# First weights in four loads instead of two, and two fewer late tiles stored in halves, in a 2:4-sparse matmul

## The chip, the cores and the metric

The kernel runs on one core of one Trainium2 chip. The metric is the device time of one execution in microseconds. A core has five engines that run side by side, each with its own list of instructions: TensorE (PE; its weight loads are listed as PEld), VectorE (DVE), ScalarE (ACT), GpSimd (POOL) and SyncE (SP). SyncE and ScalarE also issue DMAs here, each through a queue of its own; the moving of bytes is done by 16 DMA engines that both queues share.

## The reference

Of every four consecutive rows of the weights, in every column, the two of largest magnitude are kept and the other two become zero; then the product with x is formed, and a bias is added.

```python
B, S, D = 16, 512, 1024            # x: B,S,D  w: D,D  b: D, all bf16
wg = w.reshape(D // 4, 4, D)
mag = jnp.abs(wg)
order = jnp.argsort(mag, 1)
thr = jnp.take_along_axis(mag, order[:, 2:3, :], 1)   # second largest of four
wp = (wg * (mag >= thr)).reshape(D, D)
return jnp.einsum("bsd,df->bsf", x, wp) + b
```

## The kernel before

There are 8192 tokens, in 64 tiles of 128 tokens. Each tile needs 16 matmuls of 128x512 (8 blocks of the 1024 inputs, 2 halves of the 1024 outputs), and one tile's result is a row block of 128x1024.

The weights are held as `w_sb[P, G, 4, Dout]`: the partition is the index of a group of four rows, `G` is 2 (inputs 0 to 511 and 512 to 1023), and the axis of length 4 has the four rows of a group, called rows 0 to 3 below. So the four rows that compete lie side by side in a partition, and VectorE compares them elementwise. `load_w(g, c0, c1, ma, mb, eng)` (L100) loads rows `ma` to `mb` of columns `c0` to `c1` on the queue `eng`. The first piece is columns 0 to 255 of group 0: L118 loads rows 0 and 1 on SyncE's queue, L119 rows 2 and 3 on ScalarE's. One row of that piece is 128 partitions x 256 columns x 2 bytes = 64 KB.

Behind these two loads come, on ScalarE's queue, x tiles 5 and 6 (L120), then a small activation that makes the engine load its table; on SyncE's queue x tiles 3 and 4 (L122), x tile 2 (L123), weights columns 256 to 511 (L124), x tiles 0 and 1 (L125), three more weight loads (L126 to L128), and then the first DMA transpose, `load_lead` (L129), that brings later tiles in transposed form.

The work of the first microseconds follows an order written out by hand, one list for each engine (L266 to L289). On TensorE the list begins after 20 filler matmuls on constants (6 of 512 columns and 14 of 128, `filler`, L138), with the transposes `T3a T4a T5a T6a T2a` (L193, four matmuls each), then the matmuls `M3.0yp ...` of tiles 3 to 6 with the first piece of pruned weights (L229; `y` are rows 2 and 3, `p` and `q` the two halves of the columns), then `T0a`, `T1a` and the other pieces. On VectorE it begins with `abs0a abs0b`, the absolute values of rows 0 and 1 and then of rows 2 and 3 (L169); `hi`, `lo`, `t1`, `t2`, `thr` find the threshold, `mask` and `mult` (L159) make the pruned weights `wp`. ScalarE copies the transposed x out of the accumulator banks (`C3a ...`, L198). The dependencies along one engine are fixed by `seq`, so an engine does not run ahead of its list.

The pruned weights lie by groups of four; `spread` (L146) copies them by DMA to `wp_nat`, in the natural order of inputs, and from the first `E0` (L242) on all tiles use `wp_nat` with x that a DMA transpose has brought. After the hand-written part the other tiles run in batches of 4 and 8 (L472); the x of one batch ahead is brought by `load_nat` (L411).

A tile's result is evicted by VectorE with the bias, in two halves (`evac`), to a buffer `o`, and stored through ScalarE's queue. A tile below `NT - LATE` is stored in one DMA of 256 KB after its second half (L495); one from `NT - LATE` on in two DMAs of 128 KB, each after its own half (L493). `LATE` is 6 (L46), so these are tiles 58 to 62; tile 63 has a branch of its own with four stores (L480 to L484). Every DMA also takes one of eight semaphores in turn, and is not issued before the DMA that last used that semaphore has landed.

Of the kernel before, what the change touches and what calls it, by code (L numbers as in the profile page):

```python
# [11 lines left out]
def kernel(  # L12
# [30 lines left out]
    STG = 8  # L43
    SOLO = 6
    GROUPS = ((0, 3), (3, 6), (6, 7))
    LATE = 6  # L46
    sizes = (4, 8, 8, 8, 8, 8, 8)
    batches = []
    t0 = NPK + LEAD
# [46 lines left out]
    def issue(eng, out_, in_):  # L96
        q = nc.sync if eng == "sp" else nc.scalar
        return seq(eng, q.dma_start(out_, in_))

    def load_w(g, c0, c1, ma=0, mb=4, eng="sp"):  # L100
        issue(eng, w_sb[:, g, ma:mb, c0:c1], wv[:, g, ma:mb, c0:c1])

    def load_x(ta, tb, eng="sp"):
        xs = const.tile([P, tb - ta, HK], bf16, name=f"x_{ta}")
        issue(eng, xs[:], xf[ta * P:tb * P, :HK].rearrange("(t p) k -> p t k", p=P))
        for t in range(ta, tb):
            x_sb[t] = xs[:, t - ta, :]
# [7 lines left out]

    xnat, held = {}, {}

    load_w(0, 0, 256, 0, 2)  # L118
    load_w(0, 0, 256, 2, 4, "act")  # L119
    load_x(5, 7, "act")  # L120
    act(nc.scalar.activation(spark[:], nc.const_aps.tensor(1.0, [P, 1], bf16), Act.Abs))
    load_x(3, 5)  # L122
# [312 lines left out]
    def evac(o, ps, c0, c1, add=None):  # L435
        if add is None:
            dve(nc.vector.tensor_tensor(o[:, c0:c1], ps, bias_sb[:, c0:c1], op=Alu.add))  # L437
        else:
            dve(nc.vector.tensor_tensor(o[:, c0:c1].rearrange("p (n c) -> p n c", n=2),  # L439
                                        ps.rearrange("p (n c) -> p n c", n=2), add, op=Alu.add))  # L440
# [4 lines left out]
    def store(eng, t, o, c0=0, c1=Dout):  # L445
        issue(eng, rows(t)[:, c0:c1], o[:, c0:c1])
# [25 lines left out]
    for bi, (tb, nb) in enumerate(batches):  # L472
        if bi:
            load_batch(bi + 1)
        for j in range(nb):
# [9 lines left out]
            else:  # L485
# [4 lines left out]
                for h in range(2):  # L490
                    evac(o, pss[h][:], h * FH, (h + 1) * FH)
                    if t >= NT - LATE:
                        store("act", t, o, h * FH, (h + 1) * FH)  # L493
                if t < NT - LATE:
                    store("act", t, o)  # L495
# [30 lines left out]
```

## Time and profile before

| what | value |
|---|---|
| median of 3 runs | 232.72 us (232.28 to 232.8) |
| profiled execution, its own time | 232.89 us |
| its span, first to last instruction of the program | 231.1 us |
| HBM read, written | 3.28 MB, 16.78 MB |

The span is the part that the profile tells about; what lies around it, 1.79 us in this execution, is in the time but not in the span. Times in the views are microseconds from the start of the span. A row of the timeline has the start, the length, the engine (a `q` behind it is the engine's sequencer, which issues DMAs), the line of the code, the operation, what it writes and reads, and how many instructions were merged into the row. In brackets stands how long the engine was idle before it, and what ended that. Matmuls overlap each other, and their ends are modelled, so their pace is read from starts. A row on DMAs has what is written and read, the queue, the count, the size and the time from issue to landing. In a table by stages the columns are the stretch, its length, the busy time (and count) of PE, PEld, DVE, ACT and POOL, the granted clock, the share of the DMA engines and the GB/s that they moved.

### The profile page before, as it was taken

The numbers are of one execution on the slowest core, as the hardware profiler recorded it, in microseconds if no ns is written. First come the engines' busy times: TensorE is split into PE (matmuls) and PEld (weight loads), VectorE is DVE, ScalarE is ACT, GpSimd is POOL, SyncE is SP. The second block draws the span as 40 slices with busy tenths as digits, with TensorE's granted clock in tenths as the row PEclk, the third lists the DMA queues.
The fourth block names the chain that finished last, engine by engine and source line by source line (L and its number), as shares of the span: only waits on it lengthen the run. The fifth ranks groups of instructions, "written<-read, shape, count | busy, mean of one in ns | idle before, by whom it ended". The sixth has DMA issues, their size and how long they took to land.

```text
span 231.1 us, 2851 instructions
## 1 busy us (share of the span) xinstructions
PE 226.6 (98%) x1142; PEld 110.9 (48%) x1162; DVE 107.9 (47%) x200; ACT 14.0 (6%) x27; POOL 17.6 (8%) x15
## 2 busy tenths in 40 slices
PE   8999999999999999999999999999999999999995
PEld 5986444444444444444444444444444444444443
DVE  3999877844424424424424424423423423433434
ACT  2874100000000000000000000000000000000000
POOL 1000199700000000000000000000000000000000
PEclk9999999999999999999999999999999999999999
DMA  6999999997399422991259821693128932122122
GB/s 203 276 197 280 164 217 223 297 320 252 124 206 232 155 91 72 237 281 64 75 116 252 222 94 71 162 298 134 65 91 198 273 122 83 54 91 91 53 86 91
DMA packets 79308, 38.19 MB, mean 165 GB/s; under 512 B 64192, under 2 KB 71744, under 8 KB 79296
## 3 DMA queue, kind: packets, MB, share of 16 engines
q1 hardware_dynamic: 68384, 20.75, 43.6%
q10 hardware_dynamic: 10912, 17.27, 20.9%
q8 instruction: 9, 0.15, 0.3%
q14 instruction: 3, 0.02, 0.0%
HBM read 3.28 MB, written 16.78 MB: 87 GB/s over the span
## 4 chain that ended last, share of the span: by engine, by line
PE 98%; issue 0%; DVE 0%
PE ps L242 88%; PE ps L229 5%; PE tp L242 2%; PE ps L138 2%; PE tp L193 1%; PE ps L193 0%; DVE o L437 0%
## 5 line engine op out<-in xcount | busy, mean ns | idle before, releaser
L242 PE MATMUL ps<-wp_nat,xb 128*128 128x512 bf16 (+1 forms) x831 | 178.9, 375 | 0.9
L242 PEld LDWEIGHTS <-xb 128*128 128x128 bf16 x848 | 82.2, 98 | 97.7
L437 DVE TENSOR_TENSOR o<-ps,bias_sb 128x512 bf16<-128x512 f32 (+1 forms) x112 | 71.6, 677 | 113.7 <-PE ps L242 111.4
L433 POOL TENSOR_TENSOR st<-st,bias_sb 128x1024 f32<-128x1024 f32 x8 | 16.7, 2142 | 0.0
L242 PE MATMUL ps<-wp_nat,xlead 128*128 128x512 bf16 x63 | 14.7, 379 | 0.1
L242 PEld LDWEIGHTS <-xlead 128*128 128x128 bf16 x88 | 8.6, 98 | 10.2
L229 PE MATMUL ps<-wp,xt 128*128 128x256 bf16 (+1 forms) x130 | 12.8, 258 | 0.0
L439 DVE TENSOR_TENSOR o<-ps,st 128x512 bf16<-128x512 f32 x16 | 11.1, 691 | 2.8 <-PE ps L242 2.2
L229 PEld LDWEIGHTS <-xt 128*128 128x128 bf16 x130 | 10.9, 98 | 1.1
L242 PE MATMUL ps<-wp_nat,xlow 128*128 128x512 bf16 x47 | 10.6, 379 | 0.1
L264 ACT COPY st<-ps 128x512 f32<-128x512 f32 x14 | 7.4, 600 | 3.2 <-PE ps L229 3.1
L242 PEld LDWEIGHTS <-xlow 128*128 128x128 bf16 x48 | 4.7, 98 | 5.7
L159 DVE TENSOR_TENSOR mag<-mag,hi 128x256 bf16<-128x256 bf16 (+2 forms) x15 | 6.1, 435 | 0.1
L159 DVE TENSOR_TENSOR wp<-w_sb,mag 128x256 bf16<-128x256 bf16 (+2 forms) x15 | 6.1, 435 | 0.1
L242 PE MATMUL tp<-wp_nat,xlead 128*128 128x512 bf16 x23 | 5.8, 380 | 0.0
L138 PE MATMUL ps<-const-bfloat16-1.0 128*128 128x128 bf16 (+1 forms) x20 | 4.2, 408 | 0.8 <-PEq L510 0.8
L169 DVE TENSOR_SCALAR mag<-w_sb 128x512 uint16<-128x512 uint16 (+2 forms) x5 | 2.3, 473 | 3.5 <-DMA w_sb<-in_w_dram 3.5
L138 PEld LDWEIGHTS <-const-bfloat16-1.0 128*128 128x128 bf16 x20 | 2.3, 146 | 2.4 <-issue 2.4
L159 DVE TENSOR_TENSOR hi<-mag 128x512 bf16<-128x512 bf16 (+2 forms) x7 | 3.2, 458 | 0.1
L159 DVE TENSOR_TENSOR lo<-mag 128x512 bf16<-128x512 bf16 (+1 forms) x6 | 3.1, 509 | 0.0
L193 PEld LDWEIGHTS <-x 128*128 128x128 bf16 x28 | 2.3, 124 | 0.3 <-DMA x<-in_x_dram 0.2
L422 POOL COPY pruned<-wp 128x1 bf16<-128x1 bf16 x1 | 0.2, 187 | 26.7 <-DVE wp L159 26.7
(18 smaller groups left out, 18.8 us busy)
## 6 DMA issues: line engine op xcount, KB each, us to landing
out_dram<-o ACTq DMA_DIRECT2D x58, 256.0 KB, 2.4
wp_nat<-wp SPq DMA_DIRECT2D x14, 128.0 KB, 3.2
out_dram<-o ACTq DMA_DIRECT2D x10, 128.0 KB, 1.7
w_sb<-in_w_dram SPq DMA_DIRECT2D x2, 512.0 KB, 5.5
w_sb<-in_w_dram SPq DMA_DIRECT2D x3, 256.0 KB, 5.1
x<-in_x_dram SPq DMA_DIRECT2D x2, 256.0 KB, 4.3
x<-in_x_dram ACTq DMA_DIRECT2D x1, 256.0 KB, 4.0
bias_sb<-in_b_dram SPq DMA_DIRECT2D x1, 256.0 KB, 4.7
```

The source lines that it names most:

```text
L138: pe(nc.tensor.matmul(warm_ps[:, :rep * P], lhsT=nc.const_aps.tensor(1.0, [P, P], bf16), rhs=nc.const_aps.tensor(1.0, [P, rep * P], bf16), ...
L159: dve(nc.vector.tensor_tensor(out, a, b_, op=op))
L169: dve(nc.vector.tensor_single_scalar(mag.bitcast(u16), w_.bitcast(u16), 0x7FFF, op=Alu.bitwise_and))
L193: pe(nc.tensor.transpose(tp[:, m, :], xg[:, m, :], ident[:]))
L229: pe(nc.tensor.matmul(ps[:, c0 + d:c1 + d], lhsT=xpk[t][:, m, :], rhs=wp[:, g, m, c0:c1], start=(new and m == ms.start), stop=(left[key] = ...
L242: pe(nc.tensor.matmul(ps, lhsT=xt[:, kt - koff, :], rhs=wp_nat[:, kt, c0:c1], start=(kt == first), stop=(kt == last)))
L264: act(nc.scalar.copy(staged[(q, h)][:, at, :, :].rearrange("p t c -> p (t c)"), ps_open.pop(key)[:]))
L422: pool(nc.gpsimd.tensor_copy(out=pruned[:], in_=wp[:, 1, 3, Dout - 1:]))
L433: pool(nc.gpsimd.tensor_tensor(st[:], st[:], bias.to_broadcast([P, 2, 2, CW]), op=Alu.add))
L437: dve(nc.vector.tensor_tensor(o[:, c0:c1], ps, bias_sb[:, c0:c1], op=Alu.add))
L439: dve(nc.vector.tensor_tensor(o[:, c0:c1].rearrange("p (n c) -> p n c", n=2), ps.rearrange("p (n c) -> p n c", n=2), add, op=Alu.add))
```

## The change

The first weights are loaded in four DMAs of one row each, in the order row 0 (SyncE's queue), row 1 (ScalarE's), row 2 (SyncE's), row 3 (ScalarE's). `LATE` becomes 4, so the tiles stored in halves are 60 to 62. The count of DMAs in all is the same: two more at the start, two fewer near the end.

```diff
-    LATE = 6
+    LATE = 4
...
-    load_w(0, 0, 256, 0, 2)
-    load_w(0, 0, 256, 2, 4, "act")
+    for m in range(4):
+        load_w(0, 0, 256, m, m + 1, ("sp", "act")[m % 2])
     load_x(5, 7, "act")
     act(nc.scalar.activation(spark[:], nc.const_aps.tensor(1.0, [P, 1], bf16), Act.Abs))
     load_x(3, 5)
```

VectorE's `abs0a` reads rows 0 and 1 and so waits for two loads, one of each queue; `abs0b` reads rows 2 and 3 and waits for the two others. The lists of TensorE, VectorE and ScalarE have the same instructions in the same order as before. On SyncE's queue one more load stands ahead of x tiles 3 and 4, on ScalarE's one more ahead of x tiles 5 and 6.

## The prediction

> **What bounds the kernel now.** I read the page's head first, then the chain of waits, because 98% for one engine can still hide a stretch in which it waits.
>
> ```profile
> span 231.1 us, 2851 instructions
> PE 226.6 (98%) x1142; PEld 110.9 (48%) x1162; DVE 107.9 (47%) x200; ACT 14.0 (6%) x27; POOL 17.6 (8%) x15
> PE 98%; issue 0%; DVE 0%
> ```
>
> TensorE is the bound, and the chain that ended last is TensorE's for 98% of the span. So an edit counts only where it moves the start of TensorE's unbroken work, makes a hole in that work, or lengthens what follows its last matmul. The next view is the timeline of the first microseconds: start, length (of a merged row, from the first start to the last end), engine, tile, count.
>
> ```profile
> 0.77 4.21 PE L138 MATMUL ps<-const-bfloat16-1.0 128*128 128x512 bf16 x20 [0.77 <-PEq L510]
> 4.03 0.95 PE L138 MATMUL ps<-const-bfloat16-1.0 128*128 128x128 bf16 x7
> 4.96 1.04 PE L193 MATMUL tp<-ident,x 128*128 128x128 bf16 x8
> 5.80 0.72 PE L193 MATMUL ps<-ident,x 128*128 128x128 bf16 x8
> 6.35 0.39 PE L193 MATMUL tp<-ident,x 128*128 128x128 bf16 x4
> 6.58 1.92 PE L229 MATMUL ps<-wp,xt 128*128 128x128 bf16 x20
> 4.96 0.14 PEld L193 LDWEIGHTS <-x 128*128 128x128 bf16 x2 [0.24 <-DMA x<-in_x_dram]
> L138 PE MATMUL ps<-const-bfloat16-1.0 128*128 128x128 bf16 x1 | 0.3, 314 | 0.0
> ```
>
> Lengths of matmuls overlap, so I go by starts. The last seven of the twenty fillers span 0.95 us with a last one of 0.31, so their pitch is (0.95 - 0.31) / 6 = 0.107 us and the last begins at 4.67. The next could begin at 4.78; the first transpose (T3a) begins at 4.96. The 0.18 us between is a wait for x tiles 3 and 4, and it is the only hole that this stretch has: each later row begins where the last pitch of the one before ends. T3a's start is therefore the whole kernel's start.
>
> The pitch changes inside these rows. Eight transposes take 4.96 to 5.80, 0.105 us each; four take 6.35 to 6.58, 0.057 us each. The eight between take 0.55 us: n at 0.105 and 8 - n at 0.057 gives n = 2, so TensorE goes to its full pace at about 6.01. (The granted clock reads 1.00 all along; only the pitch shows it.) This sets a rate of exchange: if T3a starts d later and the change of pace stays at 6.01, what is lost is d of slow time, worth 0.057 / 0.105 = 0.54 d at full pace.
>
> **The change, part by part.** *The four small loads.* The issues of the first loads on the two queues, and their time from issue to landing:
>
> ```profile
> 0.73 0.45 SPq L98 DMA_DIRECT2D w_sb<-in_w_dram  x1
> 1.24 0.96 SPq L98 DMA_DIRECT2D x<-in_x_dram  x2
> 2.25 0.68 SPq L98 DMA_DIRECT2D w_sb<-in_w_dram  x1
> 2.96 0.61 SPq L98 DMA_DIRECT2D x<-in_x_dram  x1
> 0.74 0.50 ACTq L98 DMA_DIRECT2D w_sb<-in_w_dram  x1
> 1.26 0.49 ACTq L98 DMA_DIRECT2D x<-in_x_dram  x1
> w_sb<-in_w_dram SPq DMA_DIRECT2D x1, 128.0 KB, 2.7
> w_sb<-in_w_dram ACTq DMA_DIRECT2D x1, 128.0 KB, 2.9
> x<-in_x_dram SPq DMA_DIRECT2D x1, 256.0 KB, 3.7
> x<-in_x_dram ACTq DMA_DIRECT2D x1, 256.0 KB, 4.0
> ```
>
> Weights rows 0 and 1 land at 0.73 + 2.7 = 3.4 and rows 2 and 3 at 0.74 + 2.9 = 3.6; x 3-4 lands at 1.24 + 3.7 = 4.9, which is T3a's release; x 5-6 at 5.3. After the change each queue issues one DMA more ahead of its x load, and every later issue moves by one step, 1.24 - 0.73 = 0.51 us. So x 3-4 is issued at about 1.75 instead of 1.24.
>
> Does it land 0.51 later? The DMA engines, by stage (share of their time, GB/s, the last two columns):
>
> ```profile
> 2.50:2.75 0.25, 0.25 (x2) 0.08 (x1) 0.00 (x0) 0.25 (x1) 0.00 (x0) 1.00 1.07 307
> 3.00:3.25 0.25, 0.25 (x2) 0.01 (x1) 0.00 (x0) 0.24 (x2) 0.00 (x0) 1.00 0.71 223
> 3.50:4.00 0.50, 0.50 (x7) 0.50 (x6) 0.50 (x3) 0.00 (x0) 0.00 (x0) 1.00 1.09 389
> 4.50:5.00 0.50, 0.50 (x6) 0.26 (x5) 0.50 (x5) 0.00 (x0) 0.00 (x0) 1.00 1.08 357
> ```
>
> From 2.50 on they are full but for one dip, and the same bytes go in the same order. x 3-4 flies 3.7 against 2.7 for the weights ahead of it; the 128 KB more are worth 0.128 / 0.38 = 0.34 us at some 380 GB/s, so about 0.66 us of its flight is standing in line, more than the 0.51 it now arrives later. By this it lands as before. The bounds: it may land early enough for T3a at 4.78 (d = -0.18; earlier is worth nothing, the fillers run until then), or the two additional loads may be worked off one after the other, each at 0.51, for d = +1.02. The trace has no load this small at the start, so I take a value near the lower rows: d = +0.15, for a dip at 3.0 that gets a little deeper. On the path: 0.54 x 0.15 = +0.08 us.
>
> The Trainium skill speaks against the split: "DMA: Bandwidth & Descriptors", section "Rules for kernel authors", would merge small transfers, and calls those under 64 KB mostly overhead; a row here is 64 KB. Its section "Anatomy of one DMA" gives, for GpSimd's path, a fixed 2.0 us and 436 GB/s, by which halving a 128 KB load saves an estimated 0.15 us of its 2.3, while the row load behind it starts a step later; the traced 2.7 and 2.9 are above its 2.3. By that page the sum would stay near zero or turn positive, never a gain.
>
> *VectorE's chain.* Rows 0 and 1 come in halves of the bytes, perhaps 0.2 to 0.3 us sooner (64 KB at 223 to 307 GB/s); rows 2 and 3 are issued at 1.24, so they land between 3.6 (as now) and 1.24 + 2.9 = 4.1.
>
> ```profile
> 3.50 0.49 DVE L169 TENSOR_SCALAR mag<-w_sb 128x512 uint16<-128x512 uint16 x2 [3.50 <-DMA w_sb<-in_w_dram]
> 5.80 0.48 DVE L159 TENSOR_TENSOR wp<-w_sb,mag 128x256 bf16<-128x256 bf16 x2
> 7.01 0.42 DVE L169 TENSOR_SCALAR mag<-w_sb 128x1024 uint16<-128x1024 uint16 x1
> 9.29 0.48 DVE L159 TENSOR_TENSOR wp<-w_sb,mag 128x256 bf16<-128x256 bf16 x2
> 9.00 1.26 PE L229 MATMUL ps<-wp,xt 128*128 128x256 bf16 x10
> ```
>
> The second abs now starts at 3.71 (half of the first row's work after 3.50); everything of VectorE is behind it. So the chain starts its common part up to 0.4 us later, and not sooner by much. The cover: the first multiply ends at 6.08, and its first matmul begins at 6.58 because TensorE is in transposes until then, 0.5 us. For the second piece the first multiply ends at 9.57, and it is used after ten matmuls from 9.00 with a pitch of 0.11, at 10.09: 0.5 us again. An earlier first abs buys nothing, a later second one costs nothing up to 0.5. Beyond, it is one to one.
>
> *What is moved on the queues.* Landings behind: x 2, weights columns 256-511, x 0-1:
>
> ```profile
> x<-in_x_dram SPq DMA_DIRECT2D x1, 128.0 KB, 4.0
> w_sb<-in_w_dram SPq DMA_DIRECT2D x1, 256.0 KB, 4.5
> x<-in_x_dram SPq DMA_DIRECT2D x1, 256.0 KB, 5.0
> 8.33 0.39 PE L193 MATMUL tp<-ident,x 128*128 128x128 bf16 x4
> 11.53 3.50 SPq L98 DMA_DIRECT2D wp_nat<-wp  x4
> 19.30 1.03 PE L242 MATMUL tp<-wp_nat,xlead 128*128 128x512 bf16 x4
> ```
>
> x 5-6 has 5.80 - 5.3 = 0.5 us of cover, x 2 6.35 - 5.75 = 0.6, x 0-1 8.33 - 7.96 = 0.37, and the second weights land at 6.75 for a VectorE that comes at 7.01. A full step of 0.51 would open 0.14 us at x 0-1 and 0.25 us on VectorE (under its 0.5); with a late T3a the covers grow by the same. SyncE's DMA transpose and the spreads of pruned weights behind it move by up to 0.5; the spread issued from 11.53 is done well before the matmuls that read it from 19.3 on. ScalarE's queue keeps only its table load and small activation behind x 5-6, with nothing to do before its first copy at 5.6. I take 0 for all of these.
>
> *The late tiles.* LATE from 6 to 4 stores tiles 58 and 59 whole, after their second half; tiles 60 to 62 stay in halves, and tile 63 has its own branch.
>
> ```profile
> 217.85 1.29 DVE L437 TENSOR_TENSOR o<-ps,bias_sb 128x512 bf16<-128x512 f32 x2 [2.17 <-PE ps L242]
> 228.46 0.29 DVE L437 TENSOR_TENSOR o<-ps,bias_sb 128x128 bf16<-128x128 f32 x1 [0.16 <-PE ps L242]
> out_dram<-o ACTq DMA_DIRECT2D x58, 256.0 KB, 2.4
> out_dram<-o ACTq DMA_DIRECT2D x10, 128.0 KB, 1.7
> ```
>
> Tile 60 is evicted from 217.85, so tile 59's whole store is issued near 216 and lands 2.4 later, some 10 us before the last eviction. Two issues more at the front and two fewer here leave the count of DMAs, and so which semaphore each late store waits on, as it was. Worth 0; without that cover, 0.7 us.
>
> **The sum**: +0.08 + 0 + 0 + 0, rounded to +0.1 on the profiled execution's 232.89 us (231.1 of span and 1.8 around it). The median of the runs shown is 0.17 lower; on it the forecast is 232.72 + 0.1 = 232.8 us.
>
> **The rivals.**
> *B, slower: the small loads are worked off one after the other.* Then T3a starts at 4.96 + 1.02 = 5.98, almost when the pace changes: 0.54 x 1.02 = +0.55, and x 0-1 lands at 8.98 where T0a would be ready at 8.88, +0.1; VectorE, with second weights at 7.77 against 7.01, is 0.76 late and shows 0.1 to 0.3 past its 0.5 cover. Together +0.6 to +0.9, 233.5 us. It decides from d = 0.7 on. For it: the dip at 3.0, as if the loads' starts and not their bytes set the pace there. Against: 0.66 us of standing in line.
> *C, slower: the change of pace is lost.* The longer hole before T3a might keep TensorE at its slow pitch for another stretch. It first took from the fillers' start at 0.77 to 6.01, 5.2 us; a second one costs 5.2 x 0.46 = 2.4 us: 235.1. Against: the present hole did no harm. By the Trainium skill, "TensorE: Matmul & The Clock Gate", Part 1, the gate watches a window of some 3.4 us that runs free of the kernel; a missed one would be an estimated 1.6 us.
> *D, faster.* x 3-4 lands in time for T3a at 4.78, and full pace comes before it instead of at 6.01: (6.01 - 4.96) x 0.46 = 0.48 and the hole's 0.05 to 0.18, -0.5 to -0.6: 232.2 us. For it: the weights leave the queues sooner in halves, and the runs shown reach down to 232.28. Against: nothing in the diff moves the pace, and without it only -0.1 is left.
> *E, nothing of it happens*: x is bound by bytes and the split is hidden; 232.7, a part of the forecast's range.
>
> **How the numbers follow.** 0.2% of this kernel, 0.47 us, is about what a measurement can tell from no change. The forecast with E has 0.58, its own range -0.1 to +0.4 (232.6 to 233.1), all of it within 0.2%. B has 0.20 and C 0.07, both slower: 0.27. D has 0.15: faster. The range goes from D's 232.2 to a little past B's 233.5, 233.6, and leaves out C and the tails.
>
> **What would show it.** In the timeline after: SyncE's first x issue near 1.75; the first transpose between 4.8 and 5.1 and its wait on the x DMA; the pitch going from 0.105 to 0.057 near 6.0; the first abs earlier than 3.5 and the second at 3.7 to 4.1; no wait of TensorE between 6.6 and 20. The forecast is wrong if T3a starts after 5.6, if the pitch is still 0.105 beyond 7, or if the time after the last matmul grows.

## The result, and the profile after

| | before | after |
|---|---|---|
| median of 16 runs | 232.5 us (232.27 to 233.11) | 233.26 us (232.61 to 233.96) |
| ratio, 95% interval | | 1.0029 (1.0017 to 1.0041) |
| profiled execution, its span | 232.89 us, 231.1 us | 233.73 us, 231.9 us |

The change makes the kernel 0.29% slower, 0.67 us (0.4 to 0.95). The two profiled executions differ by 0.84 us. The page of the changed kernel, its head, its chain of waits, and the group of VectorE's abs:

```profile
span 231.9 us, 2871 instructions
PE 227.5 (98%) x1162; PEld 110.4 (48%) x1162; DVE 108.1 (47%) x200; ACT 13.9 (6%) x27; POOL 17.6 (8%) x15
...
PE 95%; DMA 2%; SPq 1%; issue 0%; DVE 0%
...
L169 DVE TENSOR_SCALAR mag<-w_sb 128x512 uint16<-128x512 uint16 (+2 forms) x5 | 2.4, 478 | 4.5 <-DMA w_sb<-in_w_dram 4.5
```

The chain now has a DMA and SyncE's issues in it. The timeline of TensorE's matmuls and of its weight loads (the waits are clearest on PEld), then of VectorE's first three abs:

```profile
5.62 0.64 PE L193 MATMUL tp<-ident,x 128*128 128x128 bf16 x8 [0.63 <-DMA x<-in_x_dram]
6.09 0.61 PE L193 MATMUL ps<-ident,x 128*128 128x128 bf16 x8
6.76 1.92 PE L229 MATMUL ps<-wp,xt 128*128 128x128 bf16 x20
...
5.62 0.15 PEld L193 LDWEIGHTS <-x 128*128 128x128 bf16 x2 [0.90 <-DMA x<-in_x_dram]
9.03 0.26 PEld L193 LDWEIGHTS <-x 128*128 128x128 bf16 x4 [0.63 <-DMA x<-in_x_dram]
...
2.98 0.29 DVE L169 TENSOR_SCALAR mag<-w_sb 128x512 uint16<-128x512 uint16 x1 [2.98 <-DMA w_sb<-in_w_dram]
3.66 0.29 DVE L169 TENSOR_SCALAR mag<-w_sb 128x512 uint16<-128x512 uint16 x1 [0.39 <-DMA w_sb<-in_w_dram]
8.22 0.43 DVE L169 TENSOR_SCALAR mag<-w_sb 128x1024 uint16<-128x1024 uint16 x1 [1.17 <-DMA w_sb<-in_w_dram]
...
229.27 0.29 DVE L437 TENSOR_TENSOR o<-ps,bias_sb 128x128 bf16<-128x128 f32 x1 [0.15 <-PE ps L242]
```

Three things are late. T3a starts at 5.62 instead of 4.96. T0a starts at 9.03 instead of 8.33, and waits for x 0-1. The third abs, which needs the second weights, starts at 8.22 instead of 7.01, and VectorE had nothing to do for 1.17 us. The last eviction is at 229.27 instead of 228.46, 0.81 later; from there to the end of the span it is 2.6 us in both, so nothing is lost in the tail. The first abs is 0.5 us earlier, as the change would have it, and the second only 0.05 (3.66 against 3.71).

The issues, and the flights of the second weights, of x 0-1 and of the first small loads; then the DMA engines' share:

```profile
0.73 0.86 SPq L98 DMA_DIRECT2D w_sb<-in_w_dram  x2
1.65 0.94 SPq L98 DMA_DIRECT2D x<-in_x_dram  x2
2.62 0.67 SPq L98 DMA_DIRECT2D w_sb<-in_w_dram  x1
3.34 0.61 SPq L98 DMA_DIRECT2D x<-in_x_dram  x1
w_sb<-in_w_dram SPq DMA_DIRECT2D x1, 256.0 KB, 5.6
x<-in_x_dram SPq DMA_DIRECT2D x1, 256.0 KB, 5.6
w_sb<-in_w_dram SPq DMA_DIRECT2D x2, 64.0 KB, 2.2
```

```profile
3.25:3.75 0.50, 0.50 (x6) 0.46 (x5) 0.11 (x2) 0.39 (x2) 0.00 (x0) 1.00 0.33 113
6.75:7.25 0.50, 0.50 (x13) 0.50 (x11) 0.30 (x2) 0.50 (x3) 0.00 (x0) 1.00 0.74 217
```

The second weights are issued 0.37 us later (2.62 against 2.25) and fly 1.0 us longer (5.57 against 4.55; the rows round), so they land at 8.20 instead of 6.80. x 0-1 is issued 0.38 us later (3.34 against 2.96) and lands at 8.98 instead of 7.96. The DMA engines, at 1.01 from 3.25 to 3.75 before, are there at 0.33, and have a second dip, 0.74, from 6.75 to 7.25. The kernel before has these rows for the same two stretches:

```profile
3.25:3.75 0.50, 0.50 (x6) 0.46 (x5) 0.25 (x2) 0.04 (x1) 0.00 (x0) 1.00 1.01 357
6.75:7.25 0.50, 0.50 (x11) 0.48 (x9) 0.50 (x3) 0.50 (x2) 0.00 (x0) 1.00 1.02 290
```

Which of the three late starts sets the end can't be read from one profile. The experiments were made for that.

### The profile page after: what moved, and what is told of

Its sections match the earlier page's. It is cut to its first block, busy times and chain, and to the rows that moved or that the text cites. A ratio compares the mean times of both kernels' runs of the same rounds, so it can differ in the third digit from the quotient of the medians.

```text
span 231.9 us, 2871 instructions
## 1 busy us (share of the span) xinstructions
PE 227.5 (98%) x1162; PEld 110.4 (48%) x1162; DVE 108.1 (47%) x200; ACT 13.9 (6%) x27; POOL 17.6 (8%) x15
## 4 chain that ended last, share of the span: by engine, by line
PE 95%; DMA 2%; SPq 1%; issue 0%; DVE 0%
PE ps L242 88%; PE ps L229 5%; DMA x<-in_x_dram 2%; PE tp L242 2%; SPq L98 1%; PE tp L193 0%; DVE o L437 0%; PE ps L193 0%
## 5 line engine op out<-in xcount | busy, mean ns | idle before, releaser
L242 PE MATMUL ps<-wp_nat,xb 128*128 128x512 bf16 (+2 forms) x848 | 179.8, 375 | 0.0
L193 PEld LDWEIGHTS <-x 128*128 128x128 bf16 x28 | 1.7, 115 | 1.5 <-DMA x<-in_x_dram 1.5
L193 PE MATMUL tp<-ident,x 128*128 128x128 bf16 x16 | 1.4, 222 | 1.0 <-DMA x<-in_x_dram 1.0
```

The costliest lines, as they stand in the source:

```text
L193: pe(nc.tensor.transpose(tp[:, m, :], xg[:, m, :], ident[:]))
L242: pe(nc.tensor.matmul(ps, lhsT=xt[:, kt - koff, :], rhs=wp_nat[:, kt, c0:c1], start=(kt == first), stop=(kt == last)))
```

## The experiments

Ratios are against the kernel before on the same chip. The line numbers of an edited kernel are shifted by as many lines as the edit adds or removes.

### Four loads alone, and the late tiles alone

```diff
-    load_w(0, 0, 256, 0, 2)
-    load_w(0, 0, 256, 2, 4, "act")
+    for m in range(4):
+        load_w(0, 0, 256, m, m + 1, ("sp", "act")[m % 2])
```

> The four loads of one row alone, LATE left at 6. Theory (x 0-1 and x 3-4 land late because each queue has one load more ahead of them, and TensorE waits for both): as slow as the whole change, +0.5 to +0.9 us against before (ratio 1.002 to 1.004), first transpose T3a at 5.2 to 5.7, a hole ahead of T0a with x 0-1 landing near 9.0 instead of 7.96. Rival (the late tiles cost it): no slower than before, within 0.2 us.

```diff
-    LATE = 6
+    LATE = 4
```

> LATE from 6 to 4 alone, the two first weight loads as before. Theory: the same as before, within 0.2 us, and the time from the last matmul to the end of the span unchanged at 2.9 us. Rival (late tiles): +0.5 us or more. The profile is also a second look at the first loads of before: x 3-4 landing near 4.9 and x 0-1 near 8.0 if these are no accident of one execution.

Four loads alone: 233.63 us against 232.44, ratio 1.0055 (1.0034 to 1.0077), with runs from 233.28 to 235.09; T3a at 5.49, x 0-1 landing at 8.55. That is the loss of the whole change, if anything more. LATE alone: 232.63 us, ratio 1.0008 (1.0000 to 1.0016): at most 0.4 us, and from the last eviction (228.60) to the end of its span of 231.4 it is 2.8 us, in the range of the other kernels (2.6 to 2.8). The loads make the loss.

### x 0-1 taken out of the way

```diff
     load_x(5, 7, "act")
+    load_x(0, 2, "act")
...
-    load_x(0, 2)
```

This is an edit of the changed kernel.

> The changed kernel with one load moved: x tiles 0 and 1 issued on ScalarE's queue, right behind x 5-6, instead of on SyncE's behind the second weights. Theory (the hole ahead of T0a is the larger part of the loss): x 0-1 lands before 7.5, the 0.5 us hole ahead of T0a is gone, and the time falls back by 0.3 to 0.7 us, to within +0.3 us of before. Rival 1 (the late T3a is the loss): still +0.5 us or more, with no hole at T0a. Rival 2 (the DMA engines are simply full, and x 0-1 ahead of the second weights makes those late): no hole at T0a but one later, ahead of the matmuls of the second piece, and no gain.

233.59 us, ratio 1.0056 (1.0034 to 1.0078). The hole ahead of T0a is gone and nothing is won: the late x 0-1 alone does not set the end. Its profiled execution took 235.07 us and shows something else, TensorE at its slow pitch long after T3a:

```profile
5.79 1.04 PE L193 MATMUL tp<-ident,x 128*128 128x128 bf16 x8 [0.80 <-DMA x<-in_x_dram]
6.63 1.06 PE L193 MATMUL ps<-ident,x 128*128 128x128 bf16 x8
7.48 0.63 PE L193 MATMUL tp<-ident,x 128*128 128x128 bf16 x4
...
L229 PE MATMUL ps<-wp,xt 128*128 128x128 bf16 x8 | 1.1, 311 | 0.0
```

Eight transposes take 0.84 us and eight more 0.85, a pitch of 0.106, and from 7.8 to 9.5 a matmul of 128 columns still lasts 311 ns (219 at full pace, 314 for the fillers). That is rival C of the prediction, in this execution.

### The hole ahead of T3a filled

The same kernel with eight fillers more.

```diff
-    filler(14)
+    filler(22)
```

> The kernel with four loads and x 0-1 on ScalarE's queue again, with eight small fillers more (22 instead of 14), so that TensorE works until about 5.64 instead of 4.78 and the hole ahead of T3a is nearly gone. Theory (a long hole sometimes keeps TensorE at its slow pitch for one stretch more, which made the 235.07 run and its profile with full pace only at 9.64): no run above 234.3, full pace by 7.0, median 0.2 to 0.6 us below the 233.59 of the same kernel without the fillers. Rival (the hole has nothing to do with the change of pace): as slow as without them, runs near 235 as before.

233.29 us, ratio 1.0038 (1.0026 to 1.0050), all runs between 233.17 and 233.58. The high runs did not come back, and the median fell by 0.3; with five and six runs this goes with the theory more than it proves it. In its profiled execution the additional fillers did not do what they were put in for: TensorE reached its full pace among them, at 3.7 (their pitch falls from 0.10 to 0.06 us), so they ended early, and a hole of 0.30 us is left ahead of T3a (5.22). With neither a hole ahead of T0a nor a late pace, 0.9 us are still missing.

### One queue at a time

```diff
-    load_w(0, 0, 256, 0, 2)
+    load_w(0, 0, 256, 0, 1)
     load_w(0, 0, 256, 2, 4, "act")
+    load_w(0, 0, 256, 1, 2)
```

> Three loads: row 0 and row 1 each alone on SyncE's queue, rows 2 and 3 in one load on ScalarE's, LATE 6. So SyncE's queue has its extra load and ScalarE's has none. Theory (it is the step on SyncE's own queue): x 3-4 is issued 0.4 us later and x 0-1 too, nearly the whole loss stays, +0.4 to +0.8 us. Rival (both queues share what makes the descriptors, so the count of loads decides): half of it, +0.2 to +0.4 us, x 0-1 landing half way, near 8.5.

```diff
-    load_w(0, 0, 256, 2, 4, "act")
+    load_w(0, 0, 256, 2, 3, "act")
+    load_w(0, 0, 256, 3, 4, "act")
```

> Three loads: rows 0 and 1 in one load on SyncE's queue, row 2 and row 3 each alone on ScalarE's, LATE 6: the mirror of the SyncE split. Theory (what costs is the extra step on SyncE's queue, ahead of x 3-4): x 3-4 is issued at 1.24 as before and lands near 4.9 or earlier, x 5-6 lands up to 0.5 us later and is covered by T3a and T4a; time within 0.25 us of before. Rival (the count of loads decides, through what both queues share): x 3-4 lands 0.2 to 0.4 us later though issued as before, +0.3 to +0.5 us.

The split on SyncE's queue: 233.15 us, ratio 1.0033 (1.0021 to 1.0045), a loss of the expected size. The split on ScalarE's queue: 233.32 us, ratio 1.0038 (1.0025 to 1.0050), and this fits neither side. Its timeline of TensorE and VectorE, and the flight of its second weights:

```profile
4.41 0.64 PE L194 MATMUL tp<-ident,x 128*128 128x128 bf16 x8
6.29 1.92 PE L230 MATMUL ps<-wp,xt 128*128 128x128 bf16 x20
...
7.75 0.43 DVE L170 TENSOR_SCALAR mag<-w_sb 128x1024 uint16<-128x1024 uint16 x1 [0.65 <-DMA w_sb<-in_w_dram]
228.80 0.29 DVE L438 TENSOR_TENSOR o<-ps,bias_sb 128x128 bf16<-128x128 f32 x1 [0.15 <-PE ps L243]
...
2.26 0.67 SPq L98 DMA_DIRECT2D w_sb<-in_w_dram  x1
w_sb<-in_w_dram SPq DMA_DIRECT2D x1, 256.0 KB, 5.5
```

T3a is 0.55 us earlier than in the kernel before (4.41 against 4.96; TensorE reached its full pace during the fillers, so these ended sooner), the first real matmul 0.29 earlier (6.29 against 6.58), and yet the last eviction is 0.34 later. So an early T3a does not bring an early end; the theory fell here. Two loads behind are late: the second weights, which are issued as before (2.26) and fly 5.5 us instead of 4.5, and x 0-1, which lands at 8.47 instead of 7.96, so that T0a starts at 8.52.

### A second theory: VectorE's third abs

Of each profiled execution I took the starts of the third abs, of T0a and of the last eviction. The differences are taken before rounding and are of single executions; that of the kernel before took 232.89 us, 0.39 above its median.

| kernel | third abs | T0a | last eviction | after the abs | after T0a |
|---|---|---|---|---|---|
| before | 7.01 | 8.33 | 228.46 | 221.45 | 220.13 |
| LATE alone | 6.84 | 8.47 | 228.60 | 221.76 | 220.13 |
| the change | 8.22 | 9.03 | 229.27 | 221.05 | 220.24 |
| four loads alone | 7.81 | 8.59 | 228.85 | 221.04 | 220.26 |
| split on SyncE's queue | 7.54 | 8.51 | 228.63 | 221.10 | 220.13 |
| split on ScalarE's queue | 7.75 | 8.52 | 228.80 | 221.05 | 220.28 |
| x 0-1 on ScalarE's queue, fillers | 7.73 | 8.55 | 228.78 | 221.05 | 220.23 |
| x 0-1 on ScalarE's queue, late pace | 7.97 | 10.50 | 230.63 | 222.66 | 220.13 |

Four kernels have 221.04 to 221.05 after the third abs, to 0.01 us, whatever happened to T3a and T0a. From its third abs on VectorE works without a pause through the pieces, TensorE catches up with it and waits there, and the end lies a fixed time after the abs. The other four have 220.13 after T0a: there TensorE works from T0a on without waiting for VectorE. So the end is the later of two times, the third abs plus 221.05 and T0a plus 220.13.

In the kernel before T0a sets the end, and VectorE has 221.45 - 221.05 = 0.40 us of cover. The change takes 1.21 us (8.22 - 7.01); less the cover that is 0.81, which is what the last eviction lost. But T0a is late too, at 9.03 for an x 0-1 that landed at 8.98, and would alone have put the end at 229.16, 0.70 us later than before. VectorE adds 0.11 to that. Each of the two late loads is enough for most of the loss, which is why nothing is won by taking one of them out of the way. In the split on SyncE's queue T0a sets the end, and VectorE is 0.05 us short of it. T3a waits for x 3-4 there, and TensorE's work follows it without another hole:

```profile
5.56 0.69 PE L194 MATMUL tp<-ident,x 128*128 128x128 bf16 x8 [0.58 <-DMA x<-in_x_dram]
8.51 0.39 PE L194 MATMUL tp<-ident,x 128*128 128x128 bf16 x4
```

### The second weights made late by themselves

In the kernel before two loads of SyncE's queue are swapped; the first weights, x 3-4 and x 5-6 stay.

```diff
-    load_w(0, 256, 512)
     load_x(0, 2)
+    load_w(0, 256, 512)
     load_w(0, 512, 768)
```

> The kernel before with two loads of SyncE's queue swapped: x 0-1 ahead of the second weights (columns 256 to 511). The first weights, x 3-4 and x 5-6 are issued as before. New theory (VectorE's third abs, which waits for the second weights, pins TensorE's last matmul: in six of the kernels above the last matmul starts 220.78 to 220.84 us after it): the second weights land at 7.4 to 8.2, the abs starts then instead of near 7.0, T3a stays at 4.8 to 5.0, and the kernel is 0.2 to 0.8 us slower, with the last matmul 220.8 us after that abs. Rival (T3a or x 0-1 sets the end): both are as early as before or earlier, so the time is that of before, within 0.15 us.

233.22 us, ratio 1.0029 (1.0015 to 1.0043): the loss of the change, with two loads for the first weights. (Three of its twelve runs, 234.0 to 234.3, lie apart from the others; none of them has a trace.) Its timeline:

```profile
4.78 0.65 PE L193 MATMUL tp<-ident,x 128*128 128x128 bf16 x8
7.88 0.39 PE L193 MATMUL tp<-ident,x 128*128 128x128 bf16 x4
10.43 0.73 PE L229 MATMUL ps<-wp,xt 128*128 128x128 bf16 x10 [0.63 <-DVE wp L159]
...
7.80 0.43 DVE L169 TENSOR_SCALAR mag<-w_sb 128x1024 uint16<-128x1024 uint16 x1 [0.72 <-DMA w_sb<-in_w_dram]
228.85 0.29 DVE L437 TENSOR_TENSOR o<-ps,bias_sb 128x128 bf16<-128x128 f32 x1 [0.15 <-PE ps L242]
```

T3a follows the fillers with no hole at 4.78, and TensorE's wait now stands where the mechanism says, ahead of the first matmuls of the second piece, on VectorE's `wp`. Between abs and last eviction are 221.05 us again. T0a is early here (7.88) and by itself would have put the end at 228.01, so this run shows that VectorE's lateness alone is enough.

### Two other orders

x 3-4 ahead of row 2 on SyncE's queue (the changed kernel), and all four rows in one load on SyncE's queue with x 3-4 and x 5-6 on ScalarE's (the kernel before).

```diff
+    load_w(0, 0, 256, 0, 1)
+    load_w(0, 0, 256, 1, 2, "act")
+    load_x(3, 5)
+    load_w(0, 0, 256, 2, 3)
+    load_w(0, 0, 256, 3, 4, "act")
```

> The changed kernel with x 3-4 issued ahead of row 2 on SyncE's queue (row 0, x 3-4, row 2; ScalarE's: row 1, row 3, x 5-6). Four loads as in the change, the same bytes, and all behind row 2 issued as in the changed kernel. If the late T3a is the loss: x 3-4 lands at 4.9 or earlier, T3a starts by 5.0, and the time falls by 0.4 us or more against the changed kernel, to within 0.3 us of before, unless row 2 lands after 4.2 and makes the first multiplies late. If the late x 0-1 (the hole ahead of T0a) is the loss: T3a early but the hole ahead of T0a grows by as much, and the time stays at +0.6 us.

```diff
+    load_w(0, 0, 256)
+    load_x(3, 5, "act")
     load_x(5, 7, "act")
```

> The other way: one load of all four rows of the first weights on SyncE's queue; ScalarE's queue carries x 3-4 first and x 5-6 behind it, LATE 6. Theory (T3a waits for x 3-4 and its place in its queue decides): x 3-4 is issued at 0.74 and lands before 4.5, T3a starts at 4.78 with no hole, x 0-1 is issued about 0.5 us earlier; faster than before by 0.1 to 0.3 us, if the four rows land by 4.0. Rival (rows land late instead: 512 packets in one queue and x beside them): the second abs starts after 4.2, VectorE is late by more than its 0.5 us of cover, and the time is that of before or slower.

233.81 us, ratio 1.0060 (1.0048 to 1.0072), and 233.78 us, ratio 1.0058 (1.0045 to 1.0071). In both x 3-4 comes early (T3a starts at 4.78) and rows 2 and 3 late. VectorE's abs in the first of them:

```profile
5.03 0.29 DVE L171 TENSOR_SCALAR mag<-w_sb 128x512 uint16<-128x512 uint16 x1 [1.72 <-DMA w_sb<-in_w_dram]
8.34 0.42 DVE L171 TENSOR_SCALAR mag<-w_sb 128x1024 uint16<-128x1024 uint16 x1
229.38 0.29 DVE L439 TENSOR_TENSOR o<-ps,bias_sb 128x128 bf16<-128x128 f32 x1 [0.15 <-PE ps L244]
```

Here the third abs waits for no DMA at all: it is late (8.34) because VectorE's second abs began only at 5.03, and VectorE is busy from there on. The last eviction is 221.04 us behind it (in the other kernel 8.28 and 229.32, 221.04). So VectorE's chain sets the end here, late from its start and not from the second weights, and the swap of who comes first only moves the lateness from TensorE's loads to VectorE's.

### One small load more, and eight instead of four

In the kernel before, a load of 16 KB behind rows 2 and 3 on ScalarE's queue, into a tile that nothing reads:

```diff
     load_w(0, 0, 256, 2, 4, "act")
+    extra = const.tile([P, 64], bf16)
+    issue("act", extra[:], wv[:, 0, 0, 0:64])
```

> The kernel before with one more load on ScalarE's queue, behind rows 2 and 3: 128 packets of 128 bytes, 16 KB, into a tile that nothing reads. SyncE's issues are untouched. If one DMA more is enough to make the second weights late (the count of loads, not the rows that were split): they land 0.4 us or more later than before's 6.5 to 6.8, and the kernel is 0.2 to 0.9 us slower, as with the split on ScalarE's queue alone (+0.93). If splitting the rows is what does it: within 0.2 us of before.

```diff
-    load_w(0, 0, 256, 0, 2)
-    load_w(0, 0, 256, 2, 4, "act")
+    for c in range(0, 256, 128):
+        for m in range(4):
+            load_w(0, c, c + 128, m, m + 1, ("sp", "act")[m % 2])
```

> The cost doubled: the first weights in eight loads of half a row (32 KB each), four on each queue, LATE 6. Theory (each load ahead of them on SyncE's queue moves the second weights by 0.4 us of issue and more in landing): second weights issued near 3.4 and landing at 8.8 to 9.6, +1.3 to +2.2 us in all, and TensorE's last matmul 220.8 us after the third abs. Rival (only the first extra load matters, or the loss was chance of landing): no slower than the change itself, +0.5 to +0.9 us.

The small load costs as much as the split: 233.57 us, ratio 1.0041 (1.0026 to 1.0056). But the way is another than the expected one: the third abs starts at 7.17 and the last eviction 221.75 us later, so VectorE does not set the end. T0a does (8.79, 220.13 us ahead of the last eviction). x 5-6, behind the small load, is what is late:

```profile
6.33 0.64 PE L195 MATMUL ps<-ident,x 128*128 128x128 bf16 x8 [0.80 <-DMA x<-in_x_dram]
x<-in_x_dram ACTq DMA_DIRECT2D x1, 256.0 KB, 4.5
extra<-in_w_dram ACTq DMA_DIRECT2D x1, 16.0 KB, 3.3
```

T5a starts at 6.33 instead of 5.80, and TensorE stands idle ahead of it. One DMA of 16 KB more ahead of the x loads is enough for a loss of this size, and through TensorE alone; the rows need not be split.

Eight loads: 236.07 us, ratio 1.0118 (1.0086 to 1.0151), 3.4 us where 1.3 to 2.2 were expected. The second weights are issued at 3.73 and land at 8.5, so the abs is at 8.56; but T3a starts only at 6.93 after 2.1 us without work, TensorE falls back to its slow pitch (20 matmuls from 8.19 to 11.48; the granted clock is 0.50 from 7.93 to 11.34), and the last eviction is 223.05 us behind the abs, 220.13 behind T0a (11.48). Three of the four runs lie between 235.97 and 236.29, one at 234.26.

### A try at a faster version

The kernel before with x 2 and x 5-6 swapped between the queues.

```diff
-    load_x(5, 7, "act")
+    load_x(2, 3, "act")
...
-    load_x(2, 3)
+    load_x(5, 7)
```

> A try at a faster kernel: before with x 2 and x 5-6 swapped between the queues, so that ScalarE's queue carries 128 KB less beside x 3-4, and nothing is added ahead of the second weights (still fourth on SyncE's queue). If T3a's wait for x 3-4 is worth anything: x 3-4 lands before 4.7, T3a starts at 4.78, 0.05 to 0.2 us faster than before, the second weights landing by 7.0. If not: the same within 0.15 us; if x 5-6 lands after 5.8, slower by what T5a waits.

232.87 us against 232.66, ratio 1.0005 (0.9995 to 1.0015): the same (T0a at 8.00, the last eviction 220.13 us behind it). No version here beats the kernel before.

## Why the prediction was right or wrong

The range held the time (233.26 in 232.2 to 233.6); the likeliest case, no change at 232.8, did not come, and the outcome is the side that had 0.27. The range held because it had been stretched to a rival, and not by its own forecast, which ended at 233.1.

**Right: what bounds it.** TensorE, and only the first microseconds to be changed. The tail was right too: LATE alone 1.0008, the time behind the last eviction the same within 0.15 us. That T3a's start is the whole kernel's start was too simple: T3a moved by 0.66, the first real matmul by 0.18 and the last eviction by 0.81. What the end follows is T0a, plus 220.13 us, or VectorE's third abs, plus 221.05, whichever is later.

**The step that failed: what is moved on the queues, "I take 0 for all of these".** It moved the landings by the step of the issue, 0.51 at most, which left 0.14 us at x 0-1 and 0.25 us of lateness on VectorE "under its 0.5". The second weights landed 1.40 us later with an issue only 0.37 later, the third abs started 1.21 later, and the cover was 0.40. The remaining 0.81 us is the whole loss of the profiled execution. x 0-1 landed 1.02 us later with an issue 0.38 later, and T0a started 0.70 later, which alone would have cost 0.70. The 0.5 of cover at the second piece was a fair reading; that a load behind the edited ones can be delayed by some three times its delay of issue was not in the sum.

**Mis-sized: x 3-4.** I took d = +0.15, since 0.66 us of standing in line would absorb the later issue. It was issued 0.41 later (1.65 against 1.24), and T3a moved by 0.66. The DMA engines were not kept full (0.33 of them busy from 3.25 to 3.75), so the later issue was not absorbed. The exchange of 0.54 does not apply to the profiled execution: full pace came before T3a (pitch (6.09 - 5.62) / 8 = 0.059), the first real matmul was 0.18 later, and behind it the late x 0-1 and the late third abs set the rest.

**Right in kind: rival B, 233.5 us, 0.20.** Small loads delay what stands behind them, TensorE waits for x 0-1, and VectorE runs out of cover. It priced T3a at 0.55, x 0-1 at 0.1 and VectorE at 0.1 to 0.3; in the trace T0a's start is 0.70 late and VectorE adds 0.11. The landing of x 0-1 at 8.98 is the one that was measured, but T3a at 5.98 (measured 5.62) and the second weights at 7.77 (measured 8.20) are not, so that match is in part luck. Its "one after the other" was not shown: a load on one queue alone, SyncE's or ScalarE's, costs 1.0033 and 1.0038, and both together 1.0029 to 1.0055.

**Rival C came, though not in the traced execution of this kernel.** The trace of x 0-1 moved (235.07) has it, with the slow pitch beyond 9; a run of four loads alone is as long (235.09), but has no trace that shows why. In that trace the last eviction is 222.66 - 221.05 = 1.61 us later than VectorE alone would have put it. I had priced it at 2.4 from the first stretch. The Trainium skill, "TensorE: Matmul & The Clock Gate", Part 1, has a window of some 3.4 us, by which a missed one is an estimated 1.6. The traces agree: 1.61 here, and 3.41 us at a granted clock of 0.50 with eight loads (7.93 to 11.34).

**Against the split**, the Trainium skill, "DMA: Bandwidth & Descriptors", section "Rules for kernel authors", would merge small transfers. The runs go the same way, down to half rows of 32 KB at 1.0118. The small loads themselves land quickly, 2.2 us after issue against 2.7, and still nothing is won, since the second abs waits for the last of them.

## What to carry to other kernels

A load that is split to feed its reader sooner pushes back every load behind it, and the price is paid by the reader with the least cover, which need not be the next one: list for each later load its landing and its reader's start, and size the delay from runs and not from the step of the issue. Where two engines hand work to each other, subtract a late start on each from the end over several kernels, and do it for both: in each kernel the one whose difference is at its constant sets the end, and the other's distance from its own constant is what a repair of the first could win. A start that is made earlier (here the first abs, by 0.5 us) is worth nothing while a later operand of the same chain lands when it did.

## What the runs showed of the hardware that was not expected

The second weights are late by their last parts, not as a whole. A load's semaphore takes 16 steps in the trace; for the second weights (times from the start of the span):

```
kernel                    issued   1st step   13th   16th (landed)
before                      2.25       6.05   6.44   6.80
LATE alone                  2.25       6.09   6.24   6.47
the change                  2.62       6.43   6.90   8.20
split on SyncE's queue      2.63       6.08   6.55   7.51
split on ScalarE's queue    2.26       5.89   6.23   7.73
```

The first and the thirteenth step come within 0.5 us of those of before; the last comes 0.7 to 1.7 later than in the two kernels with two loads. In the same stretch (from 4.6 to 8) the packet records hold single packets of 512 or 1024 bytes that take far longer than the usual 27 to 46 ns: up to 719 ns in the change, 872 with the split on ScalarE's queue, 1576 with four loads alone, against 322 before and 482 with LATE alone. A long packet alone does not make the second weights late: with x 2 and x 5-6 swapped there is one of 769 ns, and they land at 6.28. Why one more small load at the start makes the last parts of a load late a few microseconds later, and whether long packets are the way, the traces do not tell, and no run tested it; it stays open.

TensorE's change of pace is not tied to the start of the work: with the same fillers from 0.77 on it came near 6.0 in the kernel before, near 6.5 with LATE alone, before 5.6 in the changed kernel, and at 3.9 with the split on ScalarE's queue.
